# Talking-heads attention with two gated MLPs: POOL issues every second chunk's relayout, first values fetched ahead of the relayouts, chunk rows 12 apart, six clock-keeping matmuls for 17

## The chip, the cores and the metric

The kernel runs on one core of a Trainium2 chip. TensorE (PE) multiplies, VectorE (DVE) and ScalarE (ACT) work on its results, GpSimd (POOL) does a little arithmetic and issues DMAs, and SyncE (SP) issues DMAs only. The metric is the device time of one execution in microseconds (us); lower is better.

## The reference

Two parts follow each other. The first is attention for 2 batches, 12 heads, 448 tokens and head size 64, with a mixing of heads ahead of the softmax and another behind it:

```
scores = scale * q @ k^T
scores = einsum('bhij,hg->bgij', scores, w_pre)
attn   = exp(scores - max) / (sum + 1e-09)
attn   = einsum('bhij,hg->bgij', attn, w_post)
x      = attn @ v            # then laid out as 896 tokens x 768
```

The second is two MLPs on the 896 tokens: `silu(x @ w_gate) * (x @ w_val) @ w_out` with 1536 inner columns, and then `h = x @ w_in`, `g = h * clip(h + 3, 0, 6) / 6`, `g @ w_out` with 2048. Their weights come as 64-bit words and are converted on the chip.

## The kernel before

**Tiles, chunks and pairs.** The queries of both batches are cut into eight tiles of 98 to 120 queries (`TILES`). `scores` (matmuls on line 164, in `pqk`) computes, for one tile and two heads, queries x 448 keys; six calls make a tile. `scores_out` (line 180) copies them into `S`, DVE the even heads and ACT the odd ones; there are two `S` buffers, and tile t uses `S[t % 2]`. Mixing heads needs the heads on partitions, so the scores are laid out anew by DMAs inside the chip's memory: a tile is divided into 10 to 12 chunks (`ncc`), and a chunk takes every `ncc`-th row of `S`, ten rows in all. `relayout` (line 197) moves the first eight of them, 13 columns of heads each (12 and one of zeros), into 104 rows of the buffer `sx`: 182 KB, issued by SP. `relayout_rest` (line 204) moves the last two, 12 heads each, into rows 104 to 128: 42 KB, issued by POOL. Two chunks share one `sx` and make a pair; there are 90 chunks, 45 pairs and six `sx` buffers.

**Steps.** The loop over `i` runs one step per pair. In step i PE does the `postmix` of pair i (line 261, 56 small matmuls), the `premix` of pair i + 2 (line 215, out of `sx`), two heads of `scores` for a later tile, and, for a finished tile, `av` (line 291) and `av_rest` (line 311), which multiply with the values `v`. Beside it ACT makes exponentials (`exps`), DVE the row maxima (`row_max`) and the weights, and both copy (`attn_out`). At the end of a step stand the loads of that step, then the relayouts of all chunks whose pair is at most i + 7 and whose tile has been scored, and then rests, up to pair i + 6. So on SP a load of step i is queued behind the relayouts of the steps before it.

**What waits for what.** A `premix` waits for both relayouts and both rests of its pair. A relayout waits for the copies of its tile into `S`, and for the `premix` that last used its `sx`. The copies of tile t + 2 into `S[t % 2]` wait until the last relayout and the last rest of tile t have landed: tile 2's copies begin at step 1, tile 3's at step 7. The values of batch 0 are loaded as four blocks (`load_v`, line 112) at the ends of steps 0 to 3, and `av` of tile 0, at step 5, is the first to use them; `av` takes the first three blocks, `av_rest` the fourth.

**The start.** SP and ACT load q and k. `keep_clock` (line 493) lets PE multiply a tile of zeros whose result nobody reads, 7 times at the very start and 17 times between the scores of the first two tiles and the first `premix` (`WARM`). The four pairs placed ahead of the loop have their relayouts issued as soon as tile 0 is scored. Both tables of q and k of a batch lie in one large buffer each (`new_qk`).

**The end.** From about 193 us PE does only the products of the two MLPs; a column of `g` or `v` takes it 7.30 us.

Of the kernel before, what the change touches and what calls it, by code (L numbers as in the profile page):

```python
# [7 lines left out]
F32 = mybir.dt.float32  # L8
# [15 lines left out]
KG = 5  # L24
KI = 2 * KG
# [8 lines left out]
TILES = [  # L34
    [(0, 100, 10), (100, 120, 12), (220, 120, 12), (340, 108, 11)],
    [(0, 120, 12), (120, 120, 12), (240, 110, 11), (350, 98, 10)],
]
SQ = 45 * KI

WARM = (7, 17)  # L40

LOOK = 2

# [4 lines left out]
def kernel(  # L48
# [14 lines left out]
    nc = tc.nc  # L63
# [20 lines left out]
    big = ctx.enter_context(tc.tile_pool(name="big", bufs=4, side="right"))  # L84
# [9 lines left out]

    qs, ks, vs = {}, {}, {}

    def new_qk(b):
        qs[b] = big.tile([128, HP * SQ], F32, name=f"q{b}", tag="big")
        ks[b] = big.tile([128, HP, S], F32, name=f"k{b}", tag="big")

    def load_q(b, i0, i1):
        lo, hi = (HP * KI * sum(c for _, _, c in TILES[b][:i]) for i in (i0, i1))
        nc.sync.dma_start(out=qs[b][:, lo:hi], in_=qT[b, :, lo:hi])

    def load_k(b, c0, c1, eng=nc.sync):
        eng.dma_start(out=ks[b][:, c0:c1, :], in_=kT[b, :, c0 * S : c1 * S].rearrange("p (c j) -> p c j", j=S))

    def new_v(b):
        vs[b] = pv.tile([128, JC, H, D], F32, name=f"v{b}", tag="v")

    def load_v(b, j):
        nc.sync.dma_start(
            out=vs[b][:, j].rearrange("p h d -> p (h d)"), in_=vv[b, :, j * DM : (j + 1) * DM]
        )

    def load_q0(c0, c1, eng):
        n = TILES[0][0][2] * KI
        eng.dma_start(out=qs[0][:, c0 * n : c1 * n], in_=qT[0, :, c0 * n : c1 * n])

    new_qk(0)  # L120
    load_q0(0, 2, nc.sync)
    load_k(0, 0, 1, nc.scalar)
    load_k(0, 1, 2)
    load_q0(2, 6, nc.scalar)
    load_k(0, 2, 3)
    load_k(0, 3, 4, nc.scalar)
    load_k(0, 4, 5)
# [3 lines left out]
    nc.scalar.dma_start(out=W1, in_=w_pre)  # L131
    nc.scalar.dma_start(out=W2.rearrange("p g k -> p (g k)"), in_=w_post)
    nc.gpsimd.tensor_scalar(W1, W1, 0.125, 1.0, ALU.mult, ALU.mult)
    load_q(0, 1, 2)

    Ss = [psc.tile([128, H + 1, S], F32, name=f"S{i}") for i in range(2)]
    for x in Ss:
# [7 lines left out]
    chunks = [(t, c) for t in range(8) for c in range(TILES[t // 4][t % 4][2])]  # L145
# [4 lines left out]
    stiles, pqk = {}, {}  # L150

    def scores(t, c, tags=("pqk", "pqk")):

        b, i = divmod(t, 4)
        n = TILES[b][i][2] * KI
        if c == 0:
            stiles[t] = Ss[t % 2]
        base = HP * KI * sum(x for _, _, x in TILES[b][:i]) + c * n
        p = [bank(f"pqk{t}_{c}_{e}", tags[e]) for e in range(2)]
        for s in range(2):  # L160
            lo, hi = 64 * s, min(64 * s + 64, n)
            for e in range(2):
                r = slice(64 * e, 64 * e + 64)
                nc.tensor.matmul(  # L164
                    p[e][lo:hi, :S],
                    lhsT=qs[b][r, base + lo : base + hi],
                    rhs=ks[b][r, c, :],
                    start=True,
                    stop=True,
                    tile_position=(64 * e, 64 * s),  # L170
                )
        for e in range(2):
            pqk[t, 2 * c + e] = p[e]

    def scores_out(t, c):
        n = TILES[t // 4][t % 4][2] * KI
        for e in range(2):
            h = 2 * c + e
            copy = nc.scalar.copy if e else nc.vector.tensor_copy
            copy(stiles[t][:n, h, :], pqk.pop((t, h))[:n, :S])  # L180

    sx = {}

    def relayout(m):

        t, c = chunks[m]  # L190
        b, i = divmod(t, 4)
        ncc = TILES[b][i][2]
        i, r = divmod(m, 2)
        if r == 0:
            sx[i] = psx.tile([128, 2, S], F32, name=f"sx{i}", tag="sx")
        rows = stiles[t][c : ncc * KI : ncc, :, :]
        nc.sync.dma_start(out=sx[i][0:104, r, :], in_=rows[:8, :, :])

    def relayout_rest(m):
        t, c = chunks[m]  # L200
        b, i = divmod(t, 4)
        ncc = TILES[b][i][2]
        rows = stiles[t][c : ncc * KI : ncc, :, :]
        nc.gpsimd.dma_start(out=sx[m // 2][104:128, m % 2, :], in_=rows[8:, :H, :])  # L204

    pre, tot, ew, wns, post, ats = {}, {}, {}, {}, {}, {}

# [281 lines left out]
    def keep_clock(n):  # L489

        p = ps.tile([128, 512], F32, name=f"clock{n}", tag="ppost", bufs=BUFS["ppost"])
        for _ in range(n):
            nc.tensor.matmul(p[:, :480], lhsT=idle[:, :128], rhs=idle, start=True, stop=True)

    keep_clock(WARM[0])
    placed = 0
    for t in range(2):
        for c in range(HP):
            scores(t, c, (("pqk", "pqk"), ("ppre", "ppre"), ("ppost", "ppost"), ("ppre", "pav"))[(6 * t + c) % 4])
            scores_out(t, c)  # L500
        if t == 0:
            load_q(0, 2, 3)
            for _ in range(8):
                relayout(placed)
                relayout_rest(placed)
                placed += 1
    keep_clock(WARM[1])
    rests = placed
    new_v(0)


    extra = {i: {"qk0": [], "S0": [], "av2": [], "out2": [], "qk": [], "av": [], "S": [], "rest0": [], "rest1": [], "out": [], "end": []} for i in range(-LOOK, NP)}
# [1 line left out]
    def at_step(i, f, *args, place="end"):  # L514
        extra[i][place].append((f, args))
# [12 lines left out]
    scored = {0: -3, 1: -3}  # L528
    for t in range(2, 8):
        scored[t] = 6 * t - 7  # L530
        for c in range(HP):
            i = scored[t] - 5 + c
            if t == 2 and c == 3:
                at_step(4, scores, t, c, place="qk0")
                at_step(4, scores_out, t, c, place="S0")
            else:
                at_step(i + (t == 2 and c < 3), qk, t, c, place="qk")

    split_at = {0: 16, 4: 38}
    for t, (begin, end) in enumerate(((5, 10), (11, 16), (17, 22), (23, 28), (29, 34), (35, 40), (41, 46))):  # L540
        busy = None
        for c in range(HP):
            i = begin + c * (end - begin + 1) // HP
            out = x_out if t < 6 else x_last
# [11 lines left out]
        if t < 6:  # L556
            step = 1 if t < 4 else 2
            i = split_at.setdefault(t, max(end + 1, split_at.get(t - 1, 0) + 4 // step))
            for part in range(4):
                at_step(i + part // step, x_split, t, part)  # L560

    at_step(4, new_qk, 1)
    at_step(13, new_v, 1)
    for b in range(2):
        at_step(scored[4 * b + 3] + 1, new_x, b)
    loads = [(j, load_v, 0, j) for j in (0, 1, 2, 3)] + [(2, load_q, 0, 3, 4), (5, load_q, 1, 0, 1)]
    loads += [(6 + n, load_k, 1, n, n + 1) for n in range(HP)]
    loads += [(13, load_q, 1, 1, 2), (19, load_q, 1, 2, 3), (25, load_q, 1, 3, 4)]
    loads += [(14 + 2 * j, load_v, 1, j) for j in range(JC)]
    loads += [(n, fetch, 0, "early") for n in (12, 14, 16)] + [(n, fetch, 1, "early") for n in (29, 30, 31)]  # L570
    for i, *load in loads:
# [15 lines left out]
    for i in range(-LOOK, NP):  # L587
        now = i
        soft = 0 <= i + 1 < NP
        if soft:  # L590
            exps(i + 1)
        run(i, "S")
        run(i, "av")
        run(i, "rest0")
        if i >= 0:
            postmix(i)
        run(i, "rest1")
        run(i, "qk0")
# [12 lines left out]
        run(i, "qk")  # L611
        run(i, "out2")
        if i == 41:
            late.close()
            pools["wp0"] = ctx.enter_context(tc.tile_pool(name="wp0", bufs=2, side="right"))
        if i in (42, 43):
            halve(i - 42)
        run(i, "end")
        while placed < NCH and placed // 2 <= i + LOOK + 5 and i > scored.get(chunks[placed][0], -4):
            relayout(placed)  # L620
            placed += 1

        while rests < placed and rests // 2 <= i + LOOK + 4 and i > scored[chunks[rests][0]]:
            relayout_rest(rests)
            rests += 1
    fill(FILL[3])
    last = [(6, 4), (6, 5)] + [(7, c) for c in range(HP)]
    for n, (t, c) in enumerate(last):
# [159 lines left out]
```

## Time and profile before

| | us |
|---|---|
| median of 3 runs | 702.42 (701.99 to 703.91) |
| profiled execution | 702.33 |
| its span, first to last instruction | 700.5 |
| attention and first products of PE, until columns follow back to back | about 208 |
| PE busy | 678.0 (97%) |
| DVE busy | 504.3 (72%) |
| ACT busy | 297.6 (42%) |
| POOL busy | 147.9 (21%) |
| mean granted clock of TensorE | 0.99 |

The share of PE is an average over a part with pauses (attention) and one without any (products). Times below are counted from the start of the span. [...] A DMA shows two times: that of its issue on the engine, and that from issue to landing.

### The profile page before, as it was taken

Reading aid. Unit: us, or ns where it says so; the run is one execution under the profiler, and the core shown is the slowest. Engines: PE = TensorE matmul, PEld = TensorE weight load, DVE = VectorE, ACT = ScalarE, POOL = GpSimd, SP = SyncE. Lnnn points to the kernel's source line nnn. Section 1 sums busy time; section 2 is a strip of 40 time slices with the busy share of each in tenths; the row PEclk is TensorE's granted clock in tenths of the full one; section 3 lists DMA queues with packets and bytes.
Section 4 is the critical chain, followed back from the end, with each engine's and each line's share of the span. In section 5 each row is a group of like instructions: output and inputs, shape, how many; then the busy total and the mean of one; then the engine's idle time right before and its main releaser. Section 6 shows DMA issues by size and latency. Waiting matters only on the chain.

```text
span 700.5 us, 16097 instructions
## 1 busy us (share of the span) xinstructions
PE 678.0 (97%) x6696; PEld 567.5 (81%) x6696; DVE 504.3 (72%) x836; ACT 297.6 (42%) x603; POOL 147.9 (21%) x179
## 2 busy tenths in 40 slices
PE   9769998999899999999999999999999999999998
PEld 3336565666589999999999999999999999999997
DVE  4447779988718888888888656668888888665550
ACT  4435676777623433334333323334455444332320
POOL 2413234542601112111211000004323422000000
PEclk9978999999999999999999999999999999999999
DMA  5574676555502433333324332232233223444420
GB/s 180 176 216 133 174 201 201 165 144 142 162 3 90 134 97 130 95 133 117 109 91 131 112 119 91 94 131 91 90 99 127 91 83 121 146 148 147 144 66 26
DMA packets 34200, 86.69 MB, mean 124 GB/s; under 512 B 9328, under 2 KB 22016, under 8 KB 34128
## 3 DMA queue, kind: packets, MB, share of 16 engines
q1 hardware_dynamic: 26208, 81.01, 36.3%
q0 software_dynamic: 7200, 3.94, 2.4%
q8 instruction: 52, 0.85, 0.5%
q10 hardware_dynamic: 720, 0.73, 0.3%
q14 instruction: 20, 0.16, 0.1%
HBM read 62.20 MB, written 2.75 MB: 93 GB/s over the span
## 4 chain that ended last, share of the span: by engine, by line
PE 87%; DMA 4%; DVE 4%; issue 2%; ACT 2%; SPq 1%; POOL 0%; ACTq 0%; POOLq 0%
PE pi L411 17%; PE pp L411 17%; PE po L411 12%; PE pv L411 11%; PE pg L411 11%; PE ppre L215 4%; PE pqk L164 4%; PE pav L291 4%; PE ppost L261 3%; DMA sx<-S 3%; PE p L411 2%; PE pav L311 2%; DMA v<-in_v_dram 2%; ACT e L236 1%; DVE nm L228 1%
## 5 line engine op out<-in xcount | busy, mean ns | idle before, releaser
L411 PE MATMUL pp<-g,hp 128*128 128x448 f32 x384 | 109.1, 365 | 0.0
L411 PE MATMUL po<-u,ho 128*128 128x448 f32 x288 | 81.7, 364 | 0.0
L652 POOL TENSOR_TENSOR g<-rl,g 128x448 fp32r<-128x448 f32 x32 | 41.7, 1323 | 169.1 <-ACT g L651 169.1
L411 PEld LDWEIGHTS pp<-g,hp 128*128 128x128 f32 x384 | 71.9, 187 | 5.8
L204 POOL DMA_DIRECT2D sx<-S x90 | 52.1, 579 | 105.3 <-issue 25.9
L236 ACT ACTIVATE e<-ppre,nm 128x448 f32<-128x448 f32 x90 | 56.3, 631 | 39.0 <-DVE nm L228 38.9
L411 PE MATMUL pi<-x2h,li 128*128 128x448 f32 x192 | 70.2, 366 | 0.0
L411 PE MATMUL pi<-x2l,hi 128*128 128x448 f32 x192 | 70.0, 364 | 0.0
L411 PE MATMUL pi<-x2h,hi 128*128 128x448 f32 x192 | 69.9, 364 | 0.0
L411 PE MATMUL pp<-g,lp 128*128 128x448 f32 x192 | 69.3, 361 | 0.0
L652 POOL TENSOR_TENSOR u<-sg,u 128x448 fp32r<-128x448 f32 x24 | 32.7, 1382 | 154.1 <-ACT u L651 154.1
L291 PEld LDWEIGHTS pav<-at,v 128*64 128x64 f32 x576 | 28.6, 138 | 36.3 <-ACT xs L334 18.3
L228 DVE TENSOR_REDUCE nm<-ppre 128x1 f32<-128x448 f32 x90 | 51.9, 617 | 7.2 <-PE ppre L215 4.9
L411 PEld LDWEIGHTS po<-u,ho 128*128 128x128 f32 x288 | 54.1, 188 | 3.8
L215 PE MATMUL ppre<-sx,W 64*64 64x448 f32 x360 | 52.9, 555 | 3.2 <-DMA sx<-S 2.8
L261 PE MATMUL ppost<-wn,e 60*64 60x60 f32 x2520 | 53.5, 224 | 1.3 <-issue 0.6
L411 PE MATMUL po<-u,lo 128*128 128x448 f32 x144 | 52.3, 363 | 0.0
L261 PEld LDWEIGHTS ppost<-wn,e 60*64 60x64 f32 x2520 | 47.0, 137 | 4.8 <-ACT at L279 1.7
L164 PE MATMUL pqk<-k,q 64*64 64x448 f32 (+3 forms) x384 | 50.7, 567 | 0.0
L411 PE MATMUL pg<-xl,hg 128*128 128x448 f32 x132 | 48.3, 366 | 0.0
L411 PE MATMUL pv<-xl,hv 128*128 128x448 f32 x132 | 48.3, 366 | 0.0
L411 PE MATMUL pg<-xh,hg 128*128 128x448 f32 x132 | 48.2, 365 | 0.0
(97 smaller groups left out, 1401.4 us busy)
## 6 DMA issues: line engine op xcount, KB each, us to landing
sx<-S SPq DMA_DIRECT2D x90, 182.0 KB
ri<-in_moe_w_in_dram SPq DMA_DIRECT2D x16, 768.0 KB
ro<-in_moe_w_out_dram SPq DMA_DIRECT2D x12, 768.0 KB
rg<-in_moe_w_gate_dram SPq DMA_DIRECT2D x11, 768.0 KB
rv<-in_moe_w_val_dram SPq DMA_DIRECT2D x11, 768.0 KB
rp<-in_moe_w_out_dram SPq DMA_DIRECT2D x12, 640.0 KB
rp<-in_moe_w_out_dram SPq DMA_DIRECT2D x6, 768.0 KB
sx<-S POOLq DMA_DIRECT2D x90, 42.0 KB, 5.4
```

Source lines behind the costliest of these rows:

```text
L164: nc.tensor.matmul(p[e][lo:hi, :S], lhsT=qs[b][r, base + lo : base + hi], rhs=ks[b][r, c, :], start=True, stop=True, tile_position=(64 * e ...
L204: nc.gpsimd.dma_start(out=sx[m // 2][104:128, m % 2, :], in_=rows[8:, :H, :])
L215: nc.tensor.matmul(p[a][64 * r : 64 * r + 64, :S], lhsT=W1[rows, :], rhs=x[rows, r, :], start=True, stop=True, tile_position=(64 * a, 64 * r),
L228: nc.vector.tensor_reduce(nm[:, a : a + 1], pre[i][a][:, :S], AX.X, ALU.max, negate=True)
L236: nc.scalar.activation(e2[a], p[a][:, :S], AF.Exp, bias=nm[:, a : a + 1], scale=1.0, accum_out=sm[:, a : a + 1])
L261: nc.tensor.matmul(p[s][64 * c : 64 * c + 64, at, :, :], lhsT=e2[a][rows, 64 * k : 64 * k + 64], rhs=wn[rows, a, :].rearrange("p (g k) -> ...
L291: nc.tensor.matmul(p[64 * e : 64 * e + 64, : 2 * n], lhsT=vs[b][:, jc, h, :], rhs=ats[t][:, 2 * jc : 2 * jc + 2, h, :n], start=jc == 0, st ...
L311: mm = nc.tensor.matmul(pavs[t, c][64 * e : 64 * e + 64, a * n : a * n + n], lhsT=vs[b][rows, JC - 1, h, :], rhs=ats[t][rows, KB - 1, h, : ...
L411: nc.tensor.matmul(p[:, :S], lhsT=wt[:, kk, :], rhs=xx, start=start, stop=stop)
L652: eng.tensor_tensor(to[1], src, to[0].bitcast(F32), ALU.subtract)
```

## The change

1. `relayout` goes to POOL's queue for the odd chunk of each pair and stays on SP's for the even one. Ninety relayouts on SP become 45 on SP and 45 on POOL, whose DMAs go from 90 (all of 24 rows) to 135 (45 of them of 104 rows).
2. Rests are issued directly behind the relayout of their chunk, which is one step earlier than before.
3. Rows of a chunk lie 12 apart in `S` in every tile (`STRIDE`); before, 10 to 12. Tiles of 10 or 11 chunks get rows that repeat a query and that nobody reads, so a tile has 118 to 120 rows.
4. q has a pool of its own with one buffer per tile, three in all (`load_q`).
5. Ahead of the relayouts SP now loads q of tile 1 and blocks 0 and 1 of v (before: q of tiles 1 and 2). The q of tile 2 is issued behind the first four relayouts, blocks 2 and 3 of v at the ends of steps 0 and 1 (before: 2 and 3).
6. `WARM` has 6 for 17. One pair of heads of tile 2 uses other banks.

```diff
-SQ = 45 * KI
-
-WARM = (7, 17)
+STRIDE = 12
+ROWS = [[STRIDE * (KI - 1) + n for _, _, n in t] for t in TILES]
+
+WARM = (7, 6)
...
+    pq = left.enter_context(tc.tile_pool(name="pq", bufs=3, side="left"))
...
-    def load_q(b, i0, i1):
-        lo, hi = (HP * KI * sum(c for _, _, c in TILES[b][:i]) for i in (i0, i1))
-        nc.sync.dma_start(out=qs[b][:, lo:hi], in_=qT[b, :, lo:hi])
+    def load_q(t, c0=0, c1=HP, eng=nc.sync):
+        b, i = divmod(t, 4)
+        n = ROWS[b][i]
+        if c0 == 0:
+            qs[t] = pq.tile([128, HP * STRIDE * KI], F32, name=f"q{t}", tag="q")
+        base = HP * sum(ROWS[b][:i])
+        eng.dma_start(out=qs[t][:, c0 * n : c1 * n], in_=qT[b, :, base + c0 * n : base + c1 * n])
...
-    load_q(0, 1, 2)
+    load_q(1)
+    new_v(0)
+    for j in range(2):
+        load_v(0, j)
...
     def scores_out(t, c):
-        n = TILES[t // 4][t % 4][2] * KI
+        n = ROWS[t // 4][t % 4]
...
         i, r = divmod(m, 2)
-        if r == 0:
+        if i not in sx:
             sx[i] = psx.tile([128, 2, S], F32, name=f"sx{i}", tag="sx")
-        rows = stiles[t][c : ncc * KI : ncc, :, :]
-        nc.sync.dma_start(out=sx[i][0:104, r, :], in_=rows[:8, :, :])
+        rows = stiles[t][c : c + 7 * STRIDE + 1 : STRIDE, :, :]
+        eng = nc.gpsimd if r else nc.sync
+        eng.dma_start(out=sx[i][0:104, r, :], in_=rows)
 
     def relayout_rest(m):
         t, c = chunks[m]
-        b, i = divmod(t, 4)
-        ncc = TILES[b][i][2]
-        rows = stiles[t][c : ncc * KI : ncc, :, :]
-        nc.gpsimd.dma_start(out=sx[m // 2][104:128, m % 2, :], in_=rows[8:, :H, :])
+        rows = stiles[t][c + 8 * STRIDE : c + 9 * STRIDE + 1 : STRIDE, :H, :]
+        nc.gpsimd.dma_start(out=sx[m // 2][104:128, m % 2, :], in_=rows)
...
         if t == 0:
-            load_q(0, 2, 3)
             for _ in range(8):
                 relayout(placed)
                 relayout_rest(placed)
                 placed += 1
     keep_clock(WARM[1])
-    rests = placed
-    new_v(0)
+    load_q(2)
...
-                at_step(4, scores, t, c, place="qk0")
+                at_step(4, scores, t, c, ("pav", "pqk"), place="qk0")
...
-    loads = [(j, load_v, 0, j) for j in (0, 1, 2, 3)] + [(2, load_q, 0, 3, 4), (5, load_q, 1, 0, 1)]
+    loads = [(j - 2, load_v, 0, j) for j in (2, 3)] + [(2, load_q, 3), (5, load_q, 4)]
...
             relayout(placed)
+            relayout_rest(placed)
             placed += 1
-
-        while rests < placed and rests // 2 <= i + LOOK + 4 and i > scored[chunks[rests][0]]:
-            relayout_rest(rests)
-            rests += 1
```

SP's queue from the last q load of the start to the last block of v of batch 0, before; `sx0` is the buffer of pair 0, `v0` holds the values of batch 0:

```order
L103 DMA q0_91<-in_q_dram 128x720 x2
L197 DMA sx0_173<-S0_107 104x1x448 x2
L197 DMA sx1_178<-S0_107 104x1x448 x2
...
L197 DMA sx6_294<-S1_108 104x1x448 x2
L112 DMA v0_259<-in_v_dram 128x768
L197 DMA sx7_350<-S1_108 104x1x448 x2
L112 DMA v0_259<-in_v_dram 128x768
L197 DMA sx8_413<-S1_108 104x1x448 x2
L112 DMA v0_259<-in_v_dram 128x768
L103 DMA q0_91<-in_q_dram 128x660
L197 DMA sx9_477<-S1_108 104x1x448 x2
L112 DMA v0_259<-in_v_dram 128x768
```

The same stretch of SP's queue after:

```order
L108 DMA q1_109<-in_q_dram 128x720
L117 DMA v0_111<-in_v_dram 128x768 x2
L200 DMA sx0_179<-S0_114 104x1x448
L200 DMA sx1_184<-S0_114 104x1x448
...
L200 DMA sx6_292<-S1_115 104x1x448
L117 DMA v0_111<-in_v_dram 128x768
L200 DMA sx7_348<-S1_115 104x1x448
L117 DMA v0_111<-in_v_dram 128x768
L200 DMA sx8_411<-S1_115 104x1x448
```

Two blocks of v stand ahead of all relayouts, the other two behind those of pair 6 and pair 7 (before: 8 and 9), and each pair has one row on SP for two.

POOL's queue at the first pairs, before:

```order
L138 MEMSET S1_108 128x448
L204 DMA sx0_173<-S0_107 24x1x448 x2
L204 DMA sx1_178<-S0_107 24x1x448 x2
L204 DMA sx2_183<-S0_107 24x1x448 x2
L204 DMA sx3_188<-S0_107 24x1x448 x2
```

And after:

```order
L142 MEMSET S1_115 128x448
L205 DMA sx0_179<-S0_114 24x1x448
L200 DMA sx0_179<-S0_114 104x1x448
L205 DMA sx0_179<-S0_114 24x1x448
L205 DMA sx1_184<-S0_114 24x1x448
L200 DMA sx1_184<-S0_114 104x1x448
L205 DMA sx1_184<-S0_114 24x1x448
```

Three DMAs a pair for two, with the whole relayout of the odd chunk between the two rests.

## Rows read from the trace of the kernel before

**Rows 1.** The chain that ended last, its longest links: start us, us, what.

```profile
40.45 11.59 DMA v<-in_v_dram
```

**Rows 2.** Timeline of PE: start us, us, work, [idle before <-what ended it].

```profile
44.19 0.56 PE L291 MATMUL pav<-at,v 128*64 128x100 f32 x8
47.26 0.39 PE L291 MATMUL pav<-at,v 128*64 128x100 f32 x4 [2.50 <-DMA v<-in_v_dram]
52.09 0.35 PE L311 MATMUL pav<-at,v 64*64 64x50 f32 x2 [4.44 <-DMA v<-in_v_dram]
```

**Rows 3.** Timeline of SP's issues, 0 to 64 us.

```profile
4.77 0.80 SPq L103 DMA_DIRECT2D q<-in_q_dram  x2
...
40.45 0.47 SPq L112 DMA_DIRECT2D v<-in_v_dram  x1
```

**Rows 4.** Windows: length, busy PE, PEld, DVE, ACT, POOL, clock, DMA share, GB/s.

```profile
27.00:44.00 17.00, 14.78 (x239) 7.37 (x238) 10.75 (x28) 8.00 (x22) 5.12 (x9) 0.90 0.79 215
44.00:58.00 14.00, 7.06 (x107) 4.09 (x104) 3.92 (x10) 3.28 (x9) 0.06 (x1) 0.63 0.44 133
```

**Rows 5.** The chain from 52 to 63 us: where steps 6 and 7 begin.

```profile
58.17 0.19 PE pav L311 x2
...
61.46 0.19 PE pav L311 x2
```

**Rows 6.** Timelines of ACT and DVE: first copies of tiles 2, 3 and 4.

```profile
32.36 0.53 ACT L180 COPY S<-pqk 120x448 f32<-120x448 f32 x1 [4.63 <-DMA sx<-S]
...
61.15 0.61 DVE L180 COPY S<-pqk 110x448 f32<-110x448 f32 x1
...
105.40 0.62 DVE L180 COPY S<-pqk 120x448 f32<-120x448 f32 x1 [1.53 <-DMA sx<-S]
```

**Rows 7.** Timeline of POOL, rests in groups.

```profile
11.61 2.51 POOL L204 DMA_DIRECT2D sx<-S  x4 [3.06 <-DVE S L180]
17.13 2.57 POOL L204 DMA_DIRECT2D sx<-S  x4 [3.01 <-issue]
...
58.53 1.24 POOL L204 DMA_DIRECT2D sx<-S  x2 [14.47 <-ACT e L236]
...
61.63 0.57 POOL L204 DMA_DIRECT2D sx<-S  x1 [0.35 <-DMA sx<-S]
```

**Rows 8.** Rests on POOL issued 11 to 14.5 us: issue to landing.

```profile
DMA to landing us min/median/max: 4.7/4.9/5.2
```

**Rows 9.** Rests on POOL issued 58 to 61.2 us.

```profile
DMA to landing us min/median/max: 2.8/3.5/4.7
```

**Rows 10.** DMA view, 0 to 10 us in 40 slices: busy tenths, GB/s.

```profile
DMA  0000000946999999999799999999999999942000
GB/s 0 0 0 0 0 0 0 78 50 185 303 378 377 389 403 401 373 331 327 308 402 381 382 374 357 339 404 403 410 373 380 415 392 403 357 184 81 0 0 0
```

**Rows 11.** Timeline of PE, 14 to 22 us: keep_clock and first premixes.

```profile
14.56 3.61 PE L493 MATMUL clock<-idle 128*128 128x480 bf16 x17
...
21.05 1.07 PE L215 MATMUL ppre<-sx,W 64*64 64x448 f32 x6 [1.02 <-DMA sx<-S]
```

**Rows 12.** Tile sx: its issues, ns min/median/max, first and last start.

```profile
L197 SPq DMA_DIRECT2D sx<-S x90: 686/808/2325, 11.0 to 178.0; - x90
L204 POOL DMA_DIRECT2D sx<-S x90: 571/573/791, 11.6 to 177.7; - x90
```

**Rows 13.** Rests on POOL issued 17 to 20 us.

```profile
DMA to landing us min/median/max: 3.8/4.0/4.5
```

**Rows 14.** Rests on POOL issued 61.5 to 72 us.

```profile
DMA to landing us min/median/max: 5.1/5.5/7.2
```

**Rows 15.** DMA view, 59 to 63 us.

```profile
DMA packets 667, 0.78 MB, mean 195 GB/s; under 512 B 283, under 2 KB 645, under 8 KB 666
```

**Rows 16.** DMA view, 79 to 86 us.

```profile
DMA packets 749, 0.92 MB, mean 131 GB/s; under 512 B 333, under 2 KB 662, under 8 KB 747
```

**Rows 17.** DMA view, 11 to 27 us, relayouts alone: busy tenths.

```profile
DMA  0102544354554544456566546664455445454555
```

More of the change, by code (lines that the diff above doesn't have):

```diff
@@ L95, with new_k @@
     qs, ks, vs = {}, {}, {}
-    def new_qk(b):
-        qs[b] = big.tile([128, HP * SQ], F32, name=f"q{b}", tag="big")
+    def new_k(b):
         ks[b] = big.tile([128, HP, S], F32, name=f"k{b}", tag="big")
-    def load_q(b, i0, i1):
-        lo, hi = (HP * KI * sum(c for _, _, c in TILES[b][:i]) for i in (i0, i1))
-        nc.sync.dma_start(out=qs[b][:, lo:hi], in_=qT[b, :, lo:hi])
+    def load_q(t, c0=0, c1=HP, eng=nc.sync):
[5 more added lines that the diff above has]
+        eng.dma_start(out=qs[t][:, c0 * n : c1 * n], in_=qT[b, :, base + c0 * n : base + c1 * n])
     def load_k(b, c0, c1, eng=nc.sync):
@@ L114, in load_v @@
         )
[L116 to L121, printed above, removed]
+    new_k(0)
+    load_q(0, 0, 2)
     load_k(0, 0, 1, nc.scalar)
     load_k(0, 1, 2)
-    load_q0(2, 6, nc.scalar)
+    load_q(0, 2, 6, nc.scalar)
     load_k(0, 2, 3)
@@ L154, in scores @@
         b, i = divmod(t, 4)
-        n = TILES[b][i][2] * KI
+        n = ROWS[b][i]
         if c == 0:
             stiles[t] = Ss[t % 2]
-        base = HP * KI * sum(x for _, _, x in TILES[b][:i]) + c * n
+        base = c * n
         p = [bank(f"pqk{t}_{c}_{e}", tags[e]) for e in range(2)]
@@ L165, in scores @@
                     p[e][lo:hi, :S],
-                    lhsT=qs[b][r, base + lo : base + hi],
+                    lhsT=qs[t][r, base + lo : base + hi],
                     rhs=ks[b][r, c, :],
@@ L190, in relayout @@
         t, c = chunks[m]
-        b, i = divmod(t, 4)
-        ncc = TILES[b][i][2]
         i, r = divmod(m, 2)
-        if r == 0:
+        if i not in sx:
             sx[i] = psx.tile([128, 2, S], F32, name=f"sx{i}", tag="sx")
-        rows = stiles[t][c : ncc * KI : ncc, :, :]
-        nc.sync.dma_start(out=sx[i][0:104, r, :], in_=rows[:8, :, :])
+        rows = stiles[t][c : c + 7 * STRIDE + 1 : STRIDE, :, :]
+        eng = nc.gpsimd if r else nc.sync
+        eng.dma_start(out=sx[i][0:104, r, :], in_=rows)
     def relayout_rest(m):
         t, c = chunks[m]
-        b, i = divmod(t, 4)
-        ncc = TILES[b][i][2]
-        rows = stiles[t][c : ncc * KI : ncc, :, :]
-        nc.gpsimd.dma_start(out=sx[m // 2][104:128, m % 2, :], in_=rows[8:, :H, :])
+        rows = stiles[t][c + 8 * STRIDE : c + 9 * STRIDE + 1 : STRIDE, :H, :]
+        nc.gpsimd.dma_start(out=sx[m // 2][104:128, m % 2, :], in_=rows)
     pre, tot, ew, wns, post, ats = {}, {}, {}, {}, {}, {}
@@ L560 @@
                 at_step(i + part // step, x_split, t, part)
-    at_step(4, new_qk, 1)
+    at_step(4, new_k, 1)
     at_step(13, new_v, 1)
@@ L565 @@
         at_step(scored[4 * b + 3] + 1, new_x, b)
-    loads = [(j, load_v, 0, j) for j in (0, 1, 2, 3)] + [(2, load_q, 0, 3, 4), (5, load_q, 1, 0, 1)]
+    loads = [(j - 2, load_v, 0, j) for j in (2, 3)] + [(2, load_q, 3), (5, load_q, 4)]
     loads += [(6 + n, load_k, 1, n, n + 1) for n in range(HP)]
-    loads += [(13, load_q, 1, 1, 2), (19, load_q, 1, 2, 3), (25, load_q, 1, 3, 4)]
+    loads += [(13, load_q, 5), (19, load_q, 6), (25, load_q, 7)]
     loads += [(14 + 2 * j, load_v, 1, j) for j in range(JC)]
@@ L742 @@
         part = []
-        for s0, n, ncc in TILES[b]:
-            perm = np.zeros(ncc * KI, int)
+        for (s0, n, ncc), rows in zip(TILES[b], ROWS[b]):
+            perm = np.zeros(rows, int)
             for c in range(ncc):
                 for kk in range(KI):
-                    perm[c + ncc * kk] = s0 + min(kk // KG * KG * ncc + c * KG + kk % KG, n - 1)
+                    perm[c + STRIDE * kk] = s0 + min(kk // KG * KG * ncc + c * KG + kk % KG, n - 1)
             part.append(by_pairs(q[b : b + 1, :, perm, :]).reshape(128, HP * len(perm)))
```

## The prediction, made before any run of the changed kernel

> **What bounds the kernel now.** I began with the share of busy time and the chain of work that ended last. From 193 us on nothing but products runs on PE, back to back, and the change does not touch them, so all of it is decided in the attention part, where PE is not always busy. There the chain has one long link that is no work: the fourth load of v, 11.6 us from its issue at 40.45 us to its landing [rows 1]. PE's timeline shows what it costs. The first eight `pav` matmuls of the first tile go at 44.19; the third row block of v lets the next four go 2.50 us later than PE was ready, and the last block holds the first `av_rest` for another 4.44 us [rows 2]. SP issues that load behind all the relayouts of the steps before it, the last v load 35 us after the last load of the start [rows 3].
>
> The stop has a second price. [...] Step 5 lasts from 52.09 [rows 2] to 58.17 us, the next one, at full clock, from there to 61.46 [rows 5], so 6.1 us against 3.3.
>
> Then I looked at who else sets the pace. A copy of tile t+2 into `S` waits until the last relayout of tile t has landed. Three such places matter: ACT waits 4.63 us and copies at 32.36 (tile 0 landed); DVE copies tile 3 at 61.15 without a wait that the row shows (tile 1 landed in time); and at 105.40 DVE had waited 1.53 us [rows 6]. From step 6 on a step takes about 3.35 us.
>
> Of POOL's queue the timeline tells a rule of this kernel that the change will meet. POOL issues four rests at 11.61, 0.6 us apiece, and the fifth only at 17.13 [rows 7]; the four landed 4.7 to 5.2 us after their issue [rows 8], so the fifth starts 0.3 us after the first landed (11.6 + 5.2 = 16.8). It is the same later: first issue 58.53, fifth 61.63 [rows 7], shortest landing 2.8 [rows 9]. POOL keeps **four transfers in flight** and no more. Before, it has two per pair of chunks; afterwards three.
>
> **The change part by part.** *Loads of v ahead of the relayouts.* The start's loads leave the DMA engines idle from 9.2 us of the span on [rows 10], and relayouts begin at 11. Two blocks of v are 786 KB; one q load of 369 KB leaves the burst for them, so it grows by 418 KB, 1.1 us at the 390 GB/s or so which it shows: it ends at 10.3 us, still before 11. Blocks two and three are now issued at steps 0 and 1, before at 2 and 3; even at the longest landing seen (11.6 us, [rows 1]) from an issue near 24 us they are there by 36, and step 5 asks for them at 44. Both waits go: 2.50 + 4.44 = **-6.9 us**. With them goes the half clock of step 5, 6.1 - 3.3 = **-2.8**. What is late next at that place is step 5's own work, which nothing else holds.
>
> *Six clock-keeping matmuls for 17.* The 17 take 3.61 us from 14.56 on; eleven fewer are 11 x 0.212 = 2.3 us of PE. But PE waits there for the first pairs' relayouts: the second premix is stopped by a transfer until 21.05 [rows 11], and the first cannot start before POOL's third transfer, issued at about 13 us, lands near 18. So the 2.3 us become idle time: **0**. The bounds: -0.2 if the pair lands at once, +1.5 if the clock falls in that hole and the two premixes and the first postmix run at half clock.
>
> *Issue times.* POOL takes 573 ns for a rest, SP 808 ns for a relayout of 104 rows [rows 12]. No row shows POOL with 104 rows. The low end is 0.57 (it depends on nothing but the instruction), the high end 0.579 x 104/24 = 2.5 us (by the row). I take 0.8, SP's for the same shape. Then a pair costs POOL 0.8 + 2 x 0.6 = 2.0 us, under the 3.35 of a step, so that the issue does not bound it; at 2.5 it would be 3.7, and it would.
>
> *Tile 0's relayouts.* Call L the time from issue to landing of a POOL transfer. Tile 0 needs POOL's 15th transfer (five pairs, three each): it is the third of the fourth group of four, so it starts at 11.6 + 3 (L + 0.3) + 1.5 and lands at 14.0 + 4L. For L the traces of POOL give 4.9 [rows 8] and 4.0 [rows 13] at the start, 3.5 at 58 us [rows 9], with only relayouts about; and 5.5 once other loads run beside them [rows 14]. The first three average 4.1; I take **4.2**. That SP's share of the relayouts is halved speaks for the lower rows; that a whole relayout is 182 KB and a rest 42 speaks for the upper. Tile 0 has then landed at 30.8, against 32.3 before [rows 6]: **-1.5** (L = 3.5: 28.0, of which PE can use no more than its idle time of 27 to 44, 2.2 us [rows 4], so -2.2; L = 5.4: +3.3).
>
> *Tile 1's relayouts* end with POOL's 33rd transfer, the first of the ninth group: 11.6 + 8 (L + 0.3) + L = 51.8 (L = 3.5: 45.5, early enough, so 0). Tile 3's first copy, at 61.15 before, would now want it at 61.15 - 6.9 - 2.8 - 1.5 = 50.0, so **+1.8**.
>
> *Later tiles.* A tile has 11.25 chunks on average, 16.9 transfers on POOL; at four in flight these take 16.9/4 x (L + 0.3) = 19.0 us, and its 5.6 steps last 18.8. That is +0.2 a tile, +1.2 for six. Against it stands that SP's queue has half as many transfers and that rows now lie 12 apart in every tile: where they do so already (59 to 63 us) the engines move 195 GB/s [rows 15], and 131 in 79 to 86, with rows 11 apart [rows 16]. I take back the wait of 1.5 us at 105.40 [rows 6]. Together **-0.3** (L = 3.5: 16.1 us a tile, so the ring costs nothing and -1.5 is left; L = 4.8: 21.5 us, +2.7 a tile).
>
> *The rest.* Tiles now have 118 to 120 rows; copies of 100 and of 120 rows take the same time, and q grows by 6%, 0.17 MB, 0.4 us on engines that have holes: 0. On POOL the x splits stand behind the new transfers; nothing reads them before the products, so 0.
>
> Before reaching for the rivals, what the transfers run on: with only relayouts in flight the engines are busy four to six tenths [rows 17], with loads nine tenths [rows 10]: about half of the engines' time is unused, and SP's relayouts queue up all the same. [...]
>
> The sum: -6.9 - 2.8 + 0 - 1.5 + 1.8 - 0.3 = **-9.7 us**. The profiled execution took 702.33 us (a span of 700.5 and 1.8 around it), the median of the runs is 702.42; so 692.6, which I give as **693**.
>
> **The rivals.** *POOL's four in flight become the bound* (slower). The place is POOL's ring from tile 1 on; the price grows with L. At L = 4.8: tile 0 +0.9, tile 1 lands at 57.2 where 52.3 is asked for, +4.9; later tiles +2.7 x 6 = 16; with the v gain of 9.7 that is +12, so 714. At 4.5 the terms are -0.3, +3.3 and +1.5 x 6 = 9, which with -9.7 is +2. It decides from about **L = 4.45** on. For it: the 5.5 us of rows 14, with loads running. Against it: those rests stood beside six SP relayouts issued one upon the other, and half of these are gone.
>
> *The 104-row issue on POOL is long* (2.5 us, by the row): a pair takes POOL 3.7 us against 3.35, 45 x 0.35 = 16 us at most, less the gain: 700 to 710. Against it: a rest takes 571 to 791 ns at all times, [rows 12], though DVE is busy for 10.75 of the 17 us of 27 to 44 [rows 4]. [...]
>
> *Only v gains.* The relayouts come no earlier than now, since they share engines, and the 2.3 us that keep_clock leaves end in a lower clock: -9.7 + 1.5 + 3 to +5, so 697 to 699.
>
> *The change does not do what it says:* v's last blocks land late all the same, because steps 0 and 1 queue them behind relayouts; then only tile 0 moves, 700 to 703. SP's halved queue speaks against it.
>
> **How the numbers follow.** The forecast, with L between 3.5 and 4.4 (688 to 697): 0.52. Only v gains (697 to 700): 0.20. The ring bounds it (703 to 716): 0.17. Long issue (700 to 710): 0.07. No v gain: 0.04. A measurement of this kernel can tell 0.3%, 2.1 us, from no change. Faster than 700.3: 0.50 of the forecast and 0.19 of the second, with a hundredth or two of the third, 0.70; within 0.3%: 0.08; slower than 704.5: 0.22. The range of 8 in 10 leaves a tenth below it (L under 3.5 throughout) and a tenth above: 687 to 706.
>
> **What would show it.** Right: no wait of PE for v near 44 us, granted clock near 1 from 40 to 60; postmix of step 6 near 48 us; POOL's issue of 104 rows under 1 us; POOL's transfers landing in 3.5 to 4.4 us; steps of 3.35 us up to 190; the first product at about 199 rather than 208 us. Wrong: `S` copies that wait for `sx` for 2 us and more at every tile change (the ring); POOL busy with issues through whole steps (the long issue); PE at a lower clock at 18 to 25 us (the six matmuls); a premix that waits for SP's relayout (v in the way at 11 us).

## The result and the profile after

The changed kernel takes 710.29 us (median of 14 runs, 706.08 to 714.44), the kernel before beside it 702.57 (14 runs, 700.46 to 706.34): a ratio of 1.0103, 95% interval 1.0077 to 1.0128. It is **slower by 1%, about 7 us**, and outside the forecast range. The profiled execution took 706.68 us, span 704.9, some 4 us less than the median. In every ratio below, runs more than 1.5% above the fastest of the same kernel are left out: three of ten in e12 (709.42 to 713.78 us), three of ten in e15 (708.08 to 715.17) and one of the kernel before (749.50); medians are of all runs.

First the chain of work that ended last, after the change (start us, us, what):

```profile
50.11 0.19 PE pav L312 x2
...
59.62 7.07 DMA sx<-S
...
75.04 1.72 DMA sx<-S
76.75 2.39 issue
...
84.29 0.20 PE pav L312 x2
...
209.87 7.49 PE p L412 x36
...
465.24 119.04 PE pi L412 x576
```

And the rows of before that the last three answer to:

```profile
86.07 0.20 PE pav L311 x2
...
208.40 7.48 PE p L411 x36
...
463.84 116.73 PE pi L411 x576
```

Step 6 begins at 50.11 us where it began at 58.17 [rows 5]: 8.1 us are won. Most of them are lost again by step 14, which begins at 84.29 against 86.07: 6.3 us, in links that are a transfer of `sx` and waits behind it. Another 3.3 us trickle away in the tiles after that, and the product `p` begins 1.5 us late (209.87 against 208.40). A further 2.3 us go in a product that the change was not meant to touch: `pi` lasts 119.04 us for 116.73. These two make 3.8 of the 4.4 us by which the spans differ.

PE's waits for `sx`, 10 to 208 us (in total, times, longest), after and then before:

```profile
PE ppre L216 <- DMA sx<-S: 5.7, 7, 2.6
```

```profile
PE ppre L215 <- DMA sx<-S: 2.8, 2, 1.7
```

The waits for `v` [rows 2] are gone; instead premixes wait for `sx` seven times for two. By stretch (busy PE, PEld, DVE, ACT, POOL, granted clock as a share of full speed, DMA share, GB/s), after:

```profile
15.00:27.00 12.00, 8.72 (x77) 3.42 (x80) 3.74 (x8) 3.01 (x8) 4.40 (x8) 0.80 0.75 206
44.00:58.00 14.00, 14.00 (x374) 8.38 (x370) 11.70 (x35) 9.66 (x29) 8.21 (x14) 1.00 0.47 140
80.00:84.00 4.00, 3.97 (x30) 1.98 (x32) 2.78 (x7) 2.09 (x7) 1.67 (x3) 0.57 0.93 261
```

And the first of these stretches before:

```profile
15.00:27.00 12.00, 10.40 (x154) 4.69 (x152) 5.43 (x14) 4.44 (x13) 5.18 (x9) 1.00 0.53 155
```

In 44 to 58 PE is busy all the time at full clock, where it was busy for 7.06 us at 0.63 [rows 4]. The price stands in 15 to 27: 8.72 us busy at 0.80, where the kernel before had 10.40 at 1.00. And the half clock that left step 5 (0.52 before, from 52.09 to 58.17 us) is back at a later place: behind the wait for tile 4's copies (below) the granted clock is 0.57 in 80 to 84 us, and eight matmuls of `pqk` last 1.49 us there for 0.75 in the next step, at 1.00. So this wait is paid twice, as the wait for `v` was, where the same eight took 1.49 us in step 5 and 0.75 in step 6.

The first copies of tiles 2, 3 and 4 into `S`, answering to [rows 6], on ACT, DVE and DVE:

```profile
35.83 0.53 ACT L184 COPY S<-pqk 120x448 f32<-120x448 f32 x1 [3.98 <-DMA sx<-S]
...
53.48 0.61 DVE L184 COPY S<-pqk 119x448 f32<-119x448 f32 x1
...
79.33 0.62 DVE L184 COPY S<-pqk 120x448 f32<-120x448 f32 x1 [2.58 <-issue]
```

Tile 2's copy comes at 35.83, 3.5 us later than before; tile 3's waits for nothing; tile 4's stood for 2.58 us, until POOL's last transfer of tile 2, issued at 75.04 us, had landed 4.0 us later.

### The profile page after: what moved, and what is told of

Read it like the earlier page. It is cut to its first block, busy times and chain, and to the rows that moved or that the text cites. A ratio compares the mean times of both kernels' runs of the same rounds, so it can differ in the third digit from the quotient of the medians.

```text
span 704.9 us, 16033 instructions
## 1 busy us (share of the span) xinstructions
PE 684.7 (97%) x6685; PEld 568.7 (81%) x6685; DVE 507.0 (72%) x836; ACT 298.2 (42%) x603; POOL 174.9 (25%) x224
## 4 chain that ended last, share of the span: by engine, by line
PE 85%; issue 4%; DMA 4%; POOL 3%; DVE 3%; ACT 1%; SPq 0%; DVEq 0%; POOLq 0%; ACTq 0%
PE pi L412 17%; PE pp L412 17%; PE po L412 12%; PE pg L412 11%; PE pv L412 11%; PE ppre L216 3%; PE pqk L168 3%; PE pav L292 3%; DMA sx<-S 3%; PE ppost L262 3%; PE p L412 2%; POOL sx L205 2%; PE pav L312 1%; POOL sx L200 1%; DMA k<-in_k_dram 1%
## 5 line engine op out<-in xcount | busy, mean ns | idle before, releaser
L216 PE MATMUL ppre<-sx,W 64*64 64x448 f32 x360 | 62.1, 567 | 7.5 <-DMA sx<-S 5.7
L168 PE MATMUL pqk<-k,q 64*64 64x448 f32 (+3 forms) x384 | 53.8, 553 | 1.2 <-DMA k<-in_k_dram 0.8
L412 PE MATMUL pg<-xh,lg 128*128 128x448 f32 x132 | 48.2, 365 | 0.0
```

Of the source, the lines that this page charges most:

```text
L168: nc.tensor.matmul(p[e][lo:hi, :S], lhsT=qs[t][r, base + lo : base + hi], rhs=ks[b][r, c, :], start=True, stop=True, tile_position=(64 * e ...
L216: nc.tensor.matmul(p[a][64 * r : 64 * r + 64, :S], lhsT=W1[rows, :], rhs=x[rows, r, :], start=True, stop=True, tile_position=(64 * a, 64 * r),
L412: nc.tensor.matmul(p[:, :S], lhsT=wt[:, kk, :], rhs=xx, start=start, stop=stop)
```

## The experiments

Each is compared with the kernel before on the same chip; "us" is the ratio less one, times 703.

| run | what | ratio (95%) | us |
|---|---|---|---|
| after | the change | 1.0103 (1.0077 to 1.0128) | +7.2 |
| e1 | after, room for 8 in flight on POOL | 1.0010 (0.9982 to 1.0038) | +0.7 |
| e2 | after, all relayouts on SP | 0.9831 (0.9781 to 0.9880) | -11.9 |
| e3 | after, odd relayouts on ACT | 1.0285 (1.0234 to 1.0337) | +20.0 |
| e4 | after, 17 matmuls | 1.0072 (1.0041 to 1.0103) | +5.1 |
| e5 | before, odd relayouts on POOL | 1.0620 (1.0572 to 1.0668) | +43.6 |
| e6 | before, early v | 0.9936 (0.9910 to 0.9962) | -4.5 |
| e7 | e2, buffers of the old size | 0.9809 (0.9776 to 0.9842) | -13.4 |
| e8 | after, q2 and v later | 1.0086 (1.0053 to 1.0119) | +6.0 |
| e9 | e1, pairs 0 to 3 on SP | 0.9997 (0.9960 to 1.0034) | -0.2 |
| e11 | e7, rows 10 to 12 apart | 0.9890 (0.9842 to 0.9937) | -7.7 |
| e12 | e1, whole pairs on a queue | 0.9926 (0.9888 to 0.9965) | -5.2 |
| e13 | after, rests on SP | 1.0199 (1.0152 to 1.0247) | +14.0 |
| e14 | e1 and e8 | 1.0032 (0.9986 to 1.0078) | +2.2 |
| e15 | e14, loads of batch 1 later | 0.9961 (0.9924 to 0.9999) | -2.7 |
| e16 | e7, loads later | 0.9799 (0.9746 to 0.9852) | -14.1 |

**All relayouts on SP (e2).** One part of the change undone.

```diff
-        eng = nc.gpsimd if r else nc.sync
+        eng = nc.sync
```

> The changed kernel with all 90 relayouts on SP again; stride 12, the early loads of v, the six matmuls stay. Theory R: POOL is back at two transfers a pair, the relayouts keep the pace they had, and only the v gain is left: 694 to 699. Theory C (loads of k, q and weights next to the relayouts, or the new stride, slow them whoever issues them): 705 or more. Theory S (what is lost is lost at the start, where steps 0 and 1 begin 2.3 and 4.0 us later than before): the start stays late, 700 to 705.

Measured 693.02 us, 19 us under the changed kernel by the ratios (17 by the medians). So POOL's half of the relayouts costs 17 to 19 us, and everything else in the change, taken together, gains 11.9. The copy of tile 2 on ACT no longer waits for `sx`:

```profile
27.44 0.53 ACT L184 COPY S<-pqk 120x448 f32<-120x448 f32 x1 [1.85 <-PE ppost L262]
```

**More room on POOL's queue (e1).**

```diff
-dynamic_dma_scratch_size=1024
+dynamic_dma_scratch_size=2048
```

> The changed kernel (median 710.3) with twice the room for POOL's descriptors (dynamic_dma_scratch_size 2048 for 1024), nothing else. Theory R (POOL's four transfers in flight hold back the relayouts of tiles 2 and later): POOL has up to eight in flight, the copies into S and the premixes of steps 9 to 14 stop waiting, and the gain of the v loads (8.1 us at step 8) is kept: 695 to 700. Theory C (the transfers of POOL share the engines with the loads of k and of weights, and no queue would be quicker): eight in flight only make each last longer, 7 us and more to landing, and the time stays at 706 to 712.

705.03 us: between the two. POOL is held back less (the engines' idle time before instructions on `sx` that the profile puts down to `issue` is 15.8 us for 50.5, that put down to a transfer of `sx` 31.5 for 27.1), but a whole relayout takes longer to land (us, min/median/max over the execution), first in e1, then in the changed kernel:

```profile
DMA to landing us min/median/max: 3.7/7.7/10.2
```

```profile
DMA to landing us min/median/max: 2.6/4.6/7.5
```

So four in flight cost 5 to 6.5 us of the 17 to 19 (by the medians, by the ratios); beyond that it is as theory C said, with room for eight each one only lasts longer. The time lies between the two theories' ranges.

**On ACT's queue (e3).**

```diff
-        eng = nc.gpsimd if r else nc.sync
+        eng = nc.scalar if r else nc.sync
```

> The changed kernel with the odd chunk's relayout on ACT's queue instead of POOL's. Theory R: there are two transfers a pair on POOL and SP's queue is halved, so relayouts come no later than before: 692 to 698; ACT pays about 0.7 us an issue and more when its queue is full, up to +4. Theory C: the engines are as full as in the changed kernel: 705 to 711.

724.82 us, slower than either. The issue on ACT (0.70 us at the median, 3.2 at most) waits for buffers and for copies, and the exponentials stand behind it: they wait eight times, 31.4 us in all, for instructions or transfers on `sx`. PE then waits for ACT (in total, times, longest):

```profile
PE ppre L216 <- ACT e L237: 14.3, 10, 3.8
```

This says nothing for or against POOL's queue; the +4 that I allowed for ACT was the wrong size.

**Seventeen matmuls (e4).**

```diff
-WARM = (7, 6)
+WARM = (7, 17)
```

> The changed kernel with 17 clock-keeping matmuls again. Theory S (the six matmuls let the clock fall, granted 0.80 in 15 to 27 us, and steps 0 and 1 start late for that): clock 1.0 in 15 to 27 us, 2 to 4 us gained, 706 to 708. Theories R and C: the first premixes wait for relayouts in any case, and what the start loses is made up or lost again at tiles 2 and 4: within 1 us of the changed kernel, 709 to 711.

709.13 us; the intervals of the ratios overlap with the changed kernel's, so the eleven matmuls are worth between nothing and 2 us. The start isn't late for lack of them: with 17 the granted clock of 15 to 27 us is 0.94 for 0.80, and the postmix of step 0 begins no earlier (24.64 us for 24.25).

**One part alone: POOL's half in the kernel before (e5).**

```diff
-        nc.sync.dma_start(out=sx[i][0:104, r, :], in_=rows[:8, :, :])
+        (nc.gpsimd if r else nc.sync).dma_start(out=sx[i][0:104, r, :], in_=rows[:8, :, :])
```

> The kernel before with one part of the change alone: the odd chunk's relayout is issued by POOL. Theory P (the move to POOL is what costs, about 17 us by the all-SP run): 708 to 720; less than 17 more than before, because SP's halved queue lets v come sooner and part of the 6.9 us of v waits goes. Theory M (POOL costs only together with the early loads of v and q that run beside the first relayouts): 698 to 704.

745.95 us, far beyond what I expected. Here the rests are still issued a step behind their relayouts, so on POOL they stand behind relayouts of later pairs, which wait for copies of a later tile or for room (waits of PE, then of POOL):

```profile
PE ppre L215 <- DMA sx<-S: 26.7, 10, 6.4
...
POOL sx L204 <- issue: 72.9, 52, 4.3
```

As I read these waits, it is the small line of the change that issues a rest together with its relayout that keeps POOL's half from costing far more; the run differs from the change in the distance of rows and the loads too, so this is not shown by itself.

**The other part alone: early v (e6).** `load_q(0, 2, 3)` goes behind the relayouts, two `load_v` ahead of them, blocks 2 and 3 to steps 0 and 1.

> The kernel before with the new order of loads alone: blocks 0 and 1 of v ahead of the relayouts, q of tile 2 behind them, blocks 2 and 3 at steps 0 and 1. If the v wait and the clock behind it are worth what the prediction's first two terms say: -9.7, so 692 to 695, and the other parts that the all-SP run kept (stride 12, six matmuls, rests a step earlier) are worth little. If those parts made a share of the all-SP gain: 695 to 699.

699.10 us, a gain of 4.5 us for the 9.7 expected. Step 6 begins at 48.30:

```profile
48.30 0.19 PE pav L314 x2
```

That is 9.9 us before its time in the kernel before [rows 5], the forecast's -6.9 - 2.8 in sum almost to the tenth; some 5 us are given back later. That tiles whose rows lie 10 or 11 apart come late probably has a share in this, as e11 below suggests.

**Where the product pi lost 2.3 us (e7).** Of the changed kernel's buffers, those that hold k, and later x and x2, have 10752 bytes a partition for 10800, since q has left them.

```diff
-        ks[b] = big.tile([128, HP, S], F32, name=f"k{b}", tag="big")
+        ks[b] = big.tile([128, HP * 450], F32, name=f"k{b}", tag="big")[:, : HP * S].rearrange("p (c j) -> p c j", j=S)
```

> The changed kernel with all relayouts on SP, and the buffers that hold k, later x and x2, at the 10800 bytes a partition that they had before the change instead of 10752. In every run with the change the product pi takes 7.44 us a column, in the kernel before 7.29, 2.3 us in all. Theory A (the place of x2 in the memory sets the pace of these matmuls): 7.29 again, and 2.3 us under the all-SP run, near 690.7. Theory B (something else in the products): 7.44 as in the all-SP run, 693.

690.05 us, and once more 690.36 (e10, a single run). The chain has `pi` at its old length:

```profile
453.86 116.71 PE pi L412 x576
```

So 48 bytes in the size of these buffers are worth 2.3 us of `pi`; the ratios of e2 and e7 agree with it (0.9831 and 0.9809), but their intervals overlap. That it is the place of x2, as theory A has it, and not of another buffer that moves along, was not tried by itself.

**Later loads (e8, e14, e15, e16).** `load_q(2)` goes to the end of step 0, blocks 2 and 3 of v a step later (e8); the same with room for eight (e14); in addition k and q of tile 4 three steps and v of batch 1 four steps later (e15); these last alone in e7, with all relayouts on SP (e16).

> The changed kernel with the load of q of tile 2 at the end of step 0 instead of behind the first four relayouts, and blocks 2 and 3 of v a step later. Theory L (with half the relayouts gone from SP's queue its loads get ahead of the relayouts they used to stand behind, and take their engines): steps 0 and 1 begin 3 to 5 us earlier than in the changed kernel and 2 to 5 us of that are kept, 705 to 708. Theory R (POOL's four in flight alone): the start gains under 1 us, 709 to 711.

> The changed kernel with both: room for eight transfers on POOL, and the load of q of tile 2 at the end of step 0 and blocks 2 and 3 of v a step later. Alone the room gave 5.3 us and the later loads 0.7. If the loads that get ahead of the relayouts cost as soon as the four in flight no longer do: 698 to 702. If neither the loads' place nor the room is what is left of the 17 us: 703 to 706.

> The run with room for eight transfers on POOL and q2 late, with the loads of the second batch late as well: q of tile 4 and k three steps, v four steps later, so that the relayouts of tile 2 (pairs 11 to 16) run without them. In 16 us of that burst every kernel so far moves about 200 GB/s; the changed kernel spends 1.4 MB of it on loads and the all-SP run 0.7. Theory L (with SP's queue halved its loads get ahead of the relayouts on POOL, at a fixed rate of the memory): tile 2 and 4 stop waiting, 696 to 701. If the loads are not it, and what POOL lands is late in any case: 704 to 708.

> The run with all relayouts on SP and the old size of the buffers (690), with q of tile 4 and k three steps and v of batch 1 four steps later. There the loads stand in one queue behind the relayouts, so moving them should do little: 687 to 692 by theory L. More than 3 us gained would say that loads beside relayouts cost in either arrangement.

709.56, 706.73, 703.32 and 689.48 us. With room for four the place of q of tile 2 and of blocks 2 and 3 of v does nothing (+6.0 for +7.2). With room for eight, moving all these loads turns e1's +0.7 into -2.7, and all on SP the later k, q and v of batch 1 change -13.4 to -14.1, which is nothing. That points to some 3 us for loads that get ahead of POOL's relayouts, but does not show it: the intervals of e1 and e15 overlap, and by the medians +1.7 us turns into -0.5, which is 2.2.

**The start, and the division (e9, e12, e13).** e9 gives POOL odd chunks only from pair 4 on; e12 gives each queue whole pairs; both with room for eight. e13 is the changed kernel with the rests on SP.

```diff
-        eng = nc.gpsimd if r else nc.sync
+        eng = nc.gpsimd if r and i >= 4 else nc.sync
```

> The run with room for eight transfers on POOL, but the odd relayouts of pairs 0 to 3 stay on SP; POOL takes them from pair 4 on. Theory O (order at the start: SP runs ahead with the even chunks of pairs 2 and 3 while POOL, with 266 of the 448 KB of each pair, is still at pair 1, so that steps 0 and 1 begin 5 us late): steps 0 to 4 begin as in the all-SP run, and 5 to 6 us are gained on the eight-transfer run's 705: 698 to 701. Theory E (POOL's share costs evenly in every tile): 1 us gained, 703 to 705.

```diff
-        eng = nc.gpsimd if r else nc.sync
+        eng = nc.gpsimd if i % 2 else nc.sync
```

> The run with room for eight transfers on POOL, and relayouts divided by pairs: both of an odd pair on POOL, both of an even pair on SP; as many of each as before. Theory O (a pair whose two halves stand in two queues is done when the later one is, and SP's half runs ahead): pair 0 is there at 16 us as in the all-SP run, step 0 begins 3 to 4 us earlier, 698 to 703. Theory B (one stream or two, the relayouts move the same 180 to 200 GB/s, and what POOL moves it moves late): no change, 703 to 707.

```diff
-        nc.gpsimd.dma_start(out=sx[m // 2][104:128, m % 2, :], in_=rows)
+        nc.sync.dma_start(out=sx[m // 2][104:128, m % 2, :], in_=rows)
```

> The changed kernel with the rests on SP: SP issues the even chunk's relayout and both rests of a pair, POOL only the odd chunk's relayout, one transfer a pair, so that its four in flight can hardly bound it. Theory N (what costs is the number of transfers that POOL carries, three a pair, each of which lands 5 to 7 us later): most of the 17 us come back, 693 to 698. Theory T (two streams of 104-row relayouts at once get in each other's way in the memory or at the engines, whoever carries the rests): 702 to 708.

e9: 704.59, no different from e1. Its steps 0 and 1 do begin early, but the copy of tile 2 then waits for pair 4, the first on POOL:

```profile
31.95 0.53 ACT L184 COPY S<-pqk 120x448 f32<-120x448 f32 x1 [6.01 <-DMA sx<-S]
```

So theory O fell as an account of the start: the cost moves to the next place that needs POOL. e12: a ratio 0.8% under e1's, some 6 us, and the intervals don't meet; by the medians (701.58 us, 3.3 under the kernel before) it is 5. That is in theory O's range, but its reason is not shown. The kept profile, of an execution of 713.33 us, has the postmix of pair 0 no earlier than e1's; first e12, then e1:

```profile
24.86 0.36 PE L262 MATMUL ppost<-wn,e 60*64 60x60 f32 x1
```

```profile
24.09 1.05 PE L262 MATMUL ppost<-wn,e 60*64 60x60 f32 x7
```

So whole pairs seem to be worth 5 to 6 us, and why is open. e13: 717.38, slower, and so a bad test: SP now issues three transfers a pair, and already in 20 to 25 us the DMA engines are busy for a third of the time only, with PE at half its clock:

```profile
20.00:25.00 5.00, 4.57 (x23) 1.56 (x27) 1.24 (x4) 1.21 (x4) 0.08 (x1) 0.50 0.35 123
```

Both of its theories stay open, since SP's three transfers are a new hindrance.

**Distance of rows (e11).** e7 with the rows of a chunk again `ncc` apart.

> The changed kernel with all relayouts on SP and the old size of the buffers, and the rows of a chunk again 10 to 12 apart as the tile has chunks. Early v alone gave 699.1, all parts but POOL 690.1. If the distance of 12 makes the difference (relayouts of tiles with 10 and 11 chunks move at 131 GB/s where others move at 195): 697 to 700. If it is the rests issued a step earlier, or the q buffers: 690 to 692.

697.18 us for 690.05: 12 apart is worth 5.7 us by the ratios, whose intervals just meet (at 0.9842). In 15 to 27 us, when mostly tile 0 (10 chunks) is laid out anew and one load of q runs beside it, e11 and then e7 move:

```profile
DMA packets 1515, 1.87 MB, mean 156 GB/s; under 512 B 688, under 2 KB 1343, under 8 KB 1515
```

```profile
DMA packets 1833, 2.40 MB, mean 200 GB/s; under 512 B 725, under 2 KB 1633, under 8 KB 1832
```

## Why the forecast was wrong, step by step

**The v loads: right.** Both waits are gone, and so is the half clock: 0.52 in step 5 before and 1.00 in step 6, and 1.00 after in 44 to 58 us, where both now lie. Step 6 begins 8.1 us early in the changed kernel and 9.9 early where v alone is moved. That v alone brings 4.5 us at the end and not 9.7 is the step after: what is won early is kept only if the later tiles come earlier too. With all relayouts on SP the kernel does reach 693.0, but by more than the v loads: the distance of rows has a share in it.

**Issue of 104 rows on POOL: 0.8 taken, 0.60 measured** (ns min/median/max, first and last start):

```profile
L200 POOL DMA_DIRECT2D sx<-S x45: 594/597/627, 12.7 to 181.0; - x45
```

It hardly depends on the rows (a rest has 573 ns [rows 12]), and the rival of the long issue is out. The longest of the 45 issues took 0.63 us.

**L, the step that failed.** I took 4.2 us from three rows of rests with little else about, and put that one value into every stretch. Over the whole execution it was not far off: the median of POOL's whole relayouts is 4.6 (above). But a whole relayout took (min/median/max, two or three landings in each), when issued at 14.5 to 27, 44 to 52 and 52 to 66 us:

```profile
DMA to landing us min/median/max: 3.4/6.6/6.6
```

```profile
DMA to landing us min/median/max: 2.6/2.7/2.8
```

```profile
DMA to landing us min/median/max: 6.2/6.9/7.5
```

With the burst over (44 to 52) it is short. In the bursts, where it counts, it is 6.6 to 6.9, more than the 5.5 that [rows 14] had shown beside loads and that I put into a rival. By the prediction's own formula a pair then takes POOL 3 x (6.9 + 0.3) / 4 = 5.4 us against a step of 3.35. POOL's timeline in the burst of tile 2:

```profile
54.59 0.57 POOL L205 DMA_DIRECT2D sx<-S  x1 [0.20 <-PE pav L312]
56.66 0.59 POOL L200 DMA_DIRECT2D sx<-S  x1 [1.50 <-issue]
59.62 0.60 POOL L205 DMA_DIRECT2D sx<-S  x1 [2.37 <-issue]
60.86 0.57 POOL L205 DMA_DIRECT2D sx<-S  x1 [0.64 <-PE pqk L168]
61.70 0.59 POOL L200 DMA_DIRECT2D sx<-S  x1 [0.27 <-issue]
64.50 0.59 POOL L205 DMA_DIRECT2D sx<-S  x1 [2.20 <-issue]
67.00 0.57 POOL L205 DMA_DIRECT2D sx<-S  x1 [1.91 <-PE ppre L216]
```

Six transfers from 54.59 to 67.00, 2.1 us each, 6.2 a pair; of POOL's idle time there 6.3 us (`issue`) fit the four in flight, and 2.8 are waits for PE. For tile 0, 14.0 + 4L with the 5.4 us that POOL's rests took at 11 to 14.5 us gives 35.6; the fifteenth transfer, issued at 30.38, landed at 35.3, and the copy came at 35.83: +3.5 us where the forecast had -1.5. Tile 1, at +1.8, came in time; the later tiles, at -0.3, are where 9.6 us went (from 8.1 early at step 6 to 1.5 late at the products).

**The formula of the four in flight met tile 0, and its rival named the place; the one value of L, and so the choice between them, was wrong.** The rival's range, 703 to 716, holds the 710.3, but partly by luck: with room for eight only 5 to 6.5 of the 17 to 19 us came back (e1), where the formula put the whole loss on the ring, and 2.3 us of `pi` stood in neither sum.

**Why L did not fall.** I reasoned that half of the engines' time was free. It was not to be had. With room for eight (e1), and with all on SP (e2), in 15 to 27 us:

```profile
DMA packets 1709, 2.41 MB, mean 201 GB/s; under 512 B 828, under 2 KB 1345, under 8 KB 1709
...
q1 hardware_dynamic: 740, 1.45, 45.2%
q0 software_dynamic: 969, 0.97, 38.6%
```

```profile
DMA packets 1808, 2.38 MB, mean 198 GB/s; under 512 B 732, under 2 KB 1598, under 8 KB 1807
...
q1 hardware_dynamic: 1078, 1.92, 47.7%
q0 software_dynamic: 729, 0.44, 15.2%
```

The same 2.4 MB in 12 us, 200 GB/s, but the queues of e1 take 84% of the engines' time for it, those of e2 63%. The rate did not rise with the share of the engines' time. How the transfers were spread over the engines no row here shows. That transfers would land sooner for the free time was my inference, and it is what failed.

If the rate is the same either way, 198 to 201 GB/s in these rows and 194 to 204 in the next, what goes first should matter. Sixteen us of the burst of tile 2, in the changed kernel and in e2 (issues with KB each, median to landing):

```profile
DMA packets 2252, 3.27 MB, mean 204 GB/s; under 512 B 813, under 2 KB 2025, under 8 KB 2249
...
k<-in_k_dram SPq DMA_DIRECT2D x5, 224.0 KB
sx<-S SPq DMA_DIRECT2D x6, 182.0 KB
sx<-S POOLq DMA_DIRECT2D x3, 182.0 KB, 6.9
sx<-S POOLq DMA_DIRECT2D x7, 42.0 KB, 6.8
```

```profile
DMA packets 2293, 3.11 MB, mean 194 GB/s; under 512 B 761, under 2 KB 2158, under 8 KB 2290
...
sx<-S SPq DMA_DIRECT2D x11, 182.0 KB
k<-in_k_dram SPq DMA_DIRECT2D x3, 224.0 KB
sx<-S POOLq DMA_DIRECT2D x9, 42.0 KB, 6.5
```

Both move 3.1 to 3.3 MB; the changed kernel issues nine relayouts and five loads of k in it, e2 eleven and three. With one queue the loads stand behind the relayouts; with SP's queue halved more of them are issued among the relayouts. Even with one queue POOL's rests take 6.5 us in this burst, so POOL's landing time there is long whoever issues the relayouts.

**What is settled of the 17 to 19 us and what is not.** Four in flight: 5 to 6.5 (e1), about a third. Pairs divided over two queues: 5 to 6 on top of e1 (e12), measured but without a shown reason. Loads that pass: 2 to 3 (e15), not clear of noise, and perhaps in part the same time. For the rest, the two streams' higher time per byte (84% against 63%) is a candidate that was only read from the rows, not tried by itself. The cause of about two thirds of the cost thus stays open.

**Terms too small or missing.** The distance of 12 was put at 1.5 us and is worth 5.7. The six matmuls, at 0 with a bound of +1.5, cost 0 to 2, and the clock did fall in 15 to 27, to 0.80. The 2.3 us of `pi` stood nowhere in the sum. Nor did the half clock behind a wait for relayouts (0.57 in 80 to 84 us), though the sum had priced the one behind `v`. The copies into `S`, at 0, were right: for 100 to 120 rows they took 609 to 626 ns on DVE and 527 to 534 on ACT before.

## What to carry to other kernels

When transfers move to a queue with few in flight, count how many of them a step needs and take the landing time from the burst in which the step waits, beside all that then runs, not from a quiet stretch (here 6.6 to 6.9 us for 2.7). A second queue gave no bandwidth here (201 GB/s for 198 in 15 to 27 us), but it took away the order of the first: five loads of k were issued in the burst of tile 2 for three, beside nine relayouts for eleven, though what that cost is not settled. And try the parts of a change apart: here the loads and the spacing of rows, without POOL's half and with the buffers' old size, make 690.05 us, 13 us less than before.

## What the runs showed that I had not expected

The pace of one product's matmuls went with the size of buffers, and so perhaps with where an operand lies, which was not tried by itself: `pi` has 16 columns of 36 matmuls and takes 119.04 us, 7.44 a column, with buffers of 10752 bytes, and 116.7, 7.29 a column, with 10800, in each of the six profiles of either kind in which it was read. In the stretch in which tile 0 is laid out anew the engines moved 156 GB/s with rows 10 apart and 200 with rows 12 apart. And POOL's half put into the kernel before, where rests are issued a step behind their relayouts, costs 44 us for the 17 to 19 that it costs in the changed one; that the rests' order is the reason was not tried.
